# Dealing a weight conversion's steps to an inversion and to the first units by another table (RWKV-7 attention and a hard-swish MLP, one core)

## The chip, the core and the metric

The kernel runs on one core of a Trainium2 chip. It uses the core's five engines: TensorE (PE) for matrix products and transposes, VectorE (DVE) and ScalarE (ACT) for elementwise work, GpSimd (POOL) for some copies and masks, and SyncE (SP), whose queue issues nearly all transfers. Each engine works through its own list of instructions in order, and waits on semaphores for the other engines. The metric is device time in microseconds: 802.33 us, the median of three runs (801.18 to 804.81).

## The reference

Two blocks follow one another. The first is an RWKV-7 recurrence over 768 positions, for 4 batches and 8 heads of width 40; the second is an MLP with the activation h * clip(h + 3, 0, 6) / 6.

```python
for t in range(S):
    y[:, :, t] = np.einsum('bhd,bhde->bhe', rt, state)
    Sa = np.einsum('bhde,bhe->bhd', state, at)
    state_decay = state * wt[:, :, None, :] - np.einsum('bhd,bhe->bhde', Sa, bt)
    state = state_decay + np.einsum('bhd,bhe->bhde', vt, kt)
...
h = x @ w_in                      # x: 3072 x 320, w_in: 320 x 2048
g = h * np.clip(h + 3.0, 0.0, 6.0) / 6.0
out = g @ w_out                   # w_out: 2048 x 320
```

The MLP's two weights are 64-bit floating-point numbers in memory[...]: the kernel rebuilds each weight in float32 from the two 32-bit halves of a double.

## The kernel before, in words

**Units.** Time is cut into blocks of 64 positions. A unit is two such blocks of one half of the batch; there are 24, and four units make a group. For a unit, `prepare` (stages W, gam, A, B, F, K, factor, E, EV) makes decayed inputs and the matrix F of a triangular system. `invert` inverts the triangular blocks of a group on VectorE by 30 rounds of a product (L738) and a sum (L744), then two transposes (L747, L752). `third_block` completes the inverse with products on TensorE (L773, L796), copied out by ScalarE (`zs` L781, `tinv` L806). `step` uses the inverse and carries the state: its stages are RT, VT, C, R, U, UT, H, sn, y, S, rS, and two moves (L995, L1000) that bring the unit's output to the MLP's layout by transfers. In the text "2U" is stage U of unit 2, and "X" and "Y" are the two third blocks of the first group.

**MLP.** `feed_forward` is a stream of products for units whose output has been moved: `expand` (L1051) writes h to two PSUM banks, ScalarE and VectorE make gt of it (L1066, L1067), and `contract` (L1092) multiplies by w_out. Its next part cannot write h before L1067 has read the last one.

**Conversion.** `load_weights` converts 20 pieces (0 to 19). A piece takes four VectorE instructions and two on ScalarE: *mask* L349, then on ScalarE the *pair* L350 and L352, and on VectorE *bits* L369, *join* L373 and, one piece later, *product* L360 with the pair's result. It is a generator: each `next(weights)` emits one of these steps (mask and pair are one). The raw doubles are loaded at L327 into places that come free as earlier pieces are done; a later load is issued at the point of the program where the piece it waits for has been finished.

**Order.** All of it is emitted in one fixed order, with no scheduler: each engine runs its instructions in program order. In the start-up the order comes from two tables. `STEPS` says after which steps of the inversion a step of the conversion is emitted; 47 steps are reached, so larger entries do nothing. `PLAN` lists the stages of the first four units and of X and Y; the number behind a stage is how many conversion steps follow its TensorE instructions, and precede its results on VectorE and ScalarE:

```python
def run(stage, steps=0, mixed=0, deals=0):
    for at in stage:
        if at == DONE:
            return
        aside(steps, mixed)
        deal(deals)
```

Between tables, `while phase[0] == 1: next(weights)` emits a product if the last step emitted was a mask. After the PLAN the second group is prepared and the rest of the run goes on by blocks, with the MLP's stream between the units' stages.

**Buffers.** The products of the stages above go to two-bank PSUM buffers taken in turn: two of the tag `pair` and, until the MLP starts, one of the tag `lent`. A stage's TensorE work waits until the one that had its buffer three turns before has been read. So 3R (L853) takes the buffer of 2U and waits for ScalarE's copy L895 of 2U; the first h takes the place of `lent` and waits for L917 of 2UT.

Of the kernel before, what the change touches and what calls it, by code (L numbers as in the profile page):

```python
# [30 lines left out]
def kernel(  # L31
# [667 lines left out]
    def in_turn(stages, order):  # L699

        for name in order:
            yield from stages[name]()
            shared[0] = None
            yield DONE
# [512 lines left out]
    stages = [step(i) for i in range(NU)]  # L1217
    chains = [in_turn(stages[0], ["RT", "VT", "C", "R"]), in_turn(stages[1], ["RT", "VT", "C"])]
    early = deque(chains[i] for i in (0, 0, 1, 1, 0, 1, 0))
    STEPS = (1, 4, 9, 11, 12, 19, 21, 24, 28, 33, 44, 61, 64)  # L1220
    n, cleared = 0, []
    while not third:
        aside(1)
        if not third:
            n += 1
            if n in STEPS:
                next(weights, None)
# [13 lines left out]
    def block(i, j):  # L1241

        if i % NU < 2:
            if j == 0:
# [3 lines left out]

    PLAN = """X X:1 0U:3 0UT:1 1R
              0sn:1 0H:3 Y:1
              1U 1UT:3 0y:1
              2RT:3 Y:1
              1sn:1 1H:1 2VT:2 0move 0move2
              1y:2 2R
              2S:3 3RT:1
              1move 1move2 2U:2 2UT:1 2C:5
              3R:3 3VT
              2rS:3 2sn:3 2H:4 3S:2  # L1260
              2y:3 3U:2 3UT:7 3C:5
              3rS 3sn:3 3H:3 2move
              3y:2 2move2

              3move
              3move2"""
    BEGIN = 10
    plan = [[x.split(":") for x in line.split()] for line in PLAN.split("\n")]
    chains = {str(i): in_turn(stages[i], [x[0][1:] for line in plan for x in line if x[0][0] == str(i)])
# [182 lines left out]
```

## Time and profile before

| | us |
|---|---|
| median of three runs | 802.33 |
| the profiled execution, its own time | 802.65 |
| its span, first to last instruction | 800.6 |
| TensorE busy (matmuls) | 734.8 |
| VectorE busy | 501.2 |
| ScalarE busy | 306.6 |
| GpSimd busy | 177.0 |
| a conversion step on VectorE: mask, bits (each) | 0.42 |
| join, product (each) | 0.69, 0.68 |
| ScalarE pair, both instructions | 1.47 |

The profile's page gives busy times and the span in slices. The trace answers finer questions: a timeline of one engine in order of time (start, duration, engine, line, operation, output and inputs, count, and in brackets the idle time before it with what ended it), the chain of work that ended last, and tables by window. "PEclk" is the clock granted to TensorE, as a share of full speed. [...]

### The profile page before, as it was taken

What the parts mean: (1) busy time and instruction counts of PE and PEld (TensorE: products, weight loads), DVE (VectorE), ACT (ScalarE), POOL (GpSimd) and SP (SyncE); (2) the same over time, 40 slices, a digit from 0 to 9 for tenths busy, and PEclk for the clock granted to TensorE, in tenths of its full rate; (3) what the DMA queues carried; (4) which work ended last, traced back from release to release, by engine and by line L of the source; (5) the groups of instructions that cost most, each with busy time, mean ns of one, the idle gap of its engine ahead of it and who ended that gap; (6) DMA issues with size and microseconds to landing.
All of it is one profiled execution on the core that took longest, in us unless ns stands there. A gap on an engine that the chain in (4) does not pass through costs nothing.

```text
span 800.6 us, 35291 instructions
## 1 busy us (share of the span) xinstructions
PE 734.8 (92%) x15832; PEld 624.2 (78%) x15832; DVE 501.2 (63%) x986; ACT 306.6 (38%) x648; POOL 177.0 (22%) x318
## 2 busy tenths in 40 slices
PE   5725878999999989999999999999999999999998
PEld 4624766878778868888888888888888888888886
DVE  7898877679555699555698445897444983322210
ACT  2345753321644424553344453324444324412111
POOL 6403012420323222223124123304122202000000
PEclk9955688999999999999999999999999999999999
DMA  9583563420233331233222233213222101110000
GB/s 122 110 190 94 130 165 58 75 49 9 44 57 68 58 57 27 53 65 56 43 44 42 44 59 62 51 30 57 46 49 47 23 18 29 30 25 13 14 19 17
DMA packets 174214, 45.02 MB, mean 56 GB/s; under 512 B 157424, under 2 KB 172784, under 8 KB 174064
## 3 DMA queue, kind: packets, MB, share of 16 engines
q1 hardware_dynamic: 169760, 42.03, 27.7%
q8 instruction: 125, 2.05, 1.1%
q10 hardware_dynamic: 4304, 0.74, 0.7%
q14 instruction: 25, 0.20, 0.1%
HBM read 34.08 MB, written 3.93 MB: 47 GB/s over the span
## 4 chain that ended last, share of the span: by engine, by line
PE 79%; DVE 8%; issue 4%; DMA 3%; SPq 2%; ACT 2%; POOL 1%; DVEq 0%; POOLq 0%; ACTq 0%
PE h L1051 27%; PE o L1092 24%; PE pair L509 4%; PE pair L969 3%; PE one L471 3%; PE pair L946 2%; PE pair L481 2%; PE pair L853 2%; PE pair L891 2%; DVE wm L552 1%; PE pair L687 1%; PE pair L927 1%; SPq L327 1%; PE pair L796 1%; PE pair L911 1%
## 5 line engine op out<-in xcount | busy, mean ns | idle before, releaser
L1051 PE MATMUL h<-xt,win 128*128 128x128 f32 (+1 forms) x2304 | 251.3, 283 | 4.7 <-DVE gt L1067 4.7
L1051 PEld LDWEIGHTS h<-xt,win 128*128 128x128 f32 (+1 forms) x2304 | 231.7, 192 | 21.7 <-DVE gt L1067 5.0
L1092 PE MATMUL o<-wout,gt 128*128 128x320 f32 x768 | 231.5, 445 | 0.0
L1092 PEld LDWEIGHTS o<-wout,gt 128*128 128x128 f32 x768 | 139.1, 191 | 50.7 <-issue 0.8
L1067 DVE SCALAR_TENSOR_TENSOR gt<-gt,h 128x512 f32<-128x512 f32 x96 | 61.9, 680 | 72.5 <-ACT gt L1066 72.1
L1066 ACT ACTIVATE gt<-h,three 128x512 f32<-128x512 f32 x96 | 62.2, 686 | 98.8 <-PE h L1051 98.4
L981 POOL TENSOR_TENSOR yg<-ys,gam 128x512 f32<-128x512 f32 x22 | 39.4, 1792 | 164.5 <-DVE ys L980 72.5
L738 DVE TENSOR_TENSOR prod<-x 128x30 f32<-128x30 f32 (+9 forms) x180 | 67.1, 373 | 8.7 <-POOL x L723 3.3
L660 POOL TENSOR_TENSOR KBt<-K,rgt 128x320 f32<-128x320 f32 x22 | 19.1, 866 | 213.0 <-ACT rgt L649 209.4
L744 DVE TENSOR_TENSOR x<-x,prod 128x30 f32<-128x30 f32 (+9 forms) x180 | 62.2, 345 | 5.4
L954 DVE TENSOR_TENSOR state<-pair,state 40x320 f32<-40x320 f32 (+1 forms) x44 | 21.5, 488 | 64.9 <-PE pair L946 38.6
L517 DVE COPY_PREDICATED score<-mask,pair 128x512 f32<-128x512 int32 x71 | 49.8, 722 | 0.9 <-PE pair L509 0.5
L980 DVE TENSOR_TENSOR ys<-pair,ys 128x512 f32<-128x512 f32 x22 | 15.2, 690 | 43.4 <-PE pair L687 22.0
L552 DVE TENSOR_TENSOR_SCAN wm<-wm,start 128x528 f32<-128x528 f32 x24 | 37.8, 1575 | 0.8
L541 DVE TENSOR_TENSOR_SCAN prods<-wm,start 128x528 f32<-128x528 f32 x24 | 30.2, 1265 | 10.1 <-ACT wm L538 10.1
L969 PE MATMUL pair<-score,KBt 64*64 64x64 f32 x1472 | 29.3, 231 | 4.2 <-DVE state L954 3.1
L831 ACT ACTIVATE RT<-pair 128x512 f32<-128x512 f32 x21 | 12.5, 597 | 52.9 <-PE pair L481 52.9
L692 ACT ACTIVATE EV<-pair 64x320 f32<-64x320 f32 x44 | 19.0, 432 | 34.3 <-PE pair L687 23.7
L969 PEld LDWEIGHTS pair<-score,KBt 64*64 64x64 f32 x1472 | 25.8, 143 | 7.0 <-DVE state L954 3.6
L806 ACT ACTIVATE tinv<-pair 32x256 f32<-32x256 f32 x48 | 18.0, 374 | 31.5 <-PE pair L796 30.9
L569 POOL COPY gam<-prods 128x256 f32<-128x256 f32 x24 | 22.6, 940 | 29.5 <-DVE prods L541 25.7
L1110 ACT ACTIVATE ob<-o 128x320 f32<-128x320 f32 x22 | 9.6, 435 | 49.4 <-PE o L1092 29.6
(262 smaller groups left out, 1060.5 us busy)
## 6 DMA issues: line engine op xcount, KB each, us to landing
V<-in_v_dram SPq DMA_DIRECT2D x96, 40.0 KB
out_dram<-ob SPq DMA_DIRECT2D x47, 80.0 KB
R<-in_r_dram SPq DMA_DIRECT2D x92, 40.0 KB
B<-in_b_dram SPq DMA_DIRECT2D x42, 80.0 KB
K<-in_k_dram SPq DMA_DIRECT2D x42, 80.0 KB
W<-in_w_dram SPq DMA_DIRECT2D x37, 80.0 KB
A<-in_a_dram SPq DMA_DIRECT2D x37, 80.0 KB
xt<-yg SPq DMA_DIRECT2D x72, 40.0 KB
```

Source lines behind the costliest of these rows:

```text
L509: nc.tensor.matmul(out=o[i][half(q), n, :], lhsT=lhs[half(i, D), n ^ (2 * q * swap), half(q)], rhs=rhs[half(i, D), n, half(q)], start=True ...
L517: nc.vector.copy_predicated(out=x[:].rearrange("p (i h) t -> p i h t", i=2), mask=mask8, data=o[2])
L541: nc.vector.tensor_tensor_scan(out=prods[:].rearrange("p r m i -> p (r m i)"), data0=wm[:, 0:SCAN], data1=start[:], initial=0.0, op0=ALU.m ...
L552: nc.vector.tensor_tensor_scan(out=back, data0=back, data1=start[:], initial=0.0, op0=ALU.mult, op1=ALU.add)
L738: nc.vector.tensor_tensor(out=pv, in0=_ap(x[:], (i + 1) * L + i, [[L, n], [0, i]]), in1=_ap(x[:], i * L, [[0, n], [1, i]]), op=ALU.mult,)
L744: nc.vector.tensor_tensor(out=rest, in0=rest, in1=pv, op=ALU.add)
L969: nc.tensor.matmul(out=y[q][half(s), pr, :], lhsT=o[name][half(q), h * D:h * D + SLOT], rhs=m[name][half(q), 4 * rs + 2 * s + j, :], start ...
L981: nc.gpsimd.tensor_tensor(out=yg[:], in0=m["ys"][:].rearrange("p r q t -> p r (q t)"), in1=o["G"][:], op=ALU.mult)
L1051: nc.tensor.matmul(out=hp[c][:, i, :], lhsT=lhsT, rhs=rhs, start=(begun[c] == 0), stop=(begun[c] == 3 * NQ - 1))
L1066: nc.scalar.activation(out=gt[:], in_=hp[c][:], func=AF.Relu, bias=three[:], scale=1.0)
L1067: nc.vector.scalar_tensor_tensor(out=gt[:], in0=gt[:], scalar=6.0, in1=hp[c][:], op0=ALU.min, op1=ALU.mult)
L1092: nc.tensor.matmul(out=op[:], lhsT=gts[c][:, n, :], rhs=wout[:, c * HJ + r * NQ + n, :], start=((split or r == 0) and c == 0 and n == 0), ...
```

## The change

Only the two tables change. The instructions are the same, and on TensorE their order is too; on VectorE and ScalarE, conversion steps stand at other places between the inversion's steps and the first units' results; on SP one load stands at another place.

```diff
-    STEPS = (1, 4, 9, 11, 12, 19, 21, 24, 28, 33, 44, 61, 64)
+    STEPS = (6, 10, 16, 18, 25, 27, 30, 44, 45, 55, 61, 64)
...
-    PLAN = """X X:1 0U:3 0UT:1 1R
-              0sn:1 0H:3 Y:1
-              1U 1UT:3 0y:1
-              2RT:3 Y:1
+    PLAN = """X X:2 0U:4 0UT:2 1R
+              0sn:2 0H:1 Y:2
+              1U 1UT:2 0y
+              2RT:1 Y:1
               1sn:1 1H:1 2VT:2 0move 0move2
               1y:2 2R
-              2S:3 3RT:1
-              1move 1move2 2U:2 2UT:1 2C:5
-              3R:3 3VT
+              2S:3 3RT:2
+              1move 1move2 2U:3 2UT:1 2C:5
+              3R:4 3VT
               2rS:3 2sn:3 2H:4 3S:2
-              2y:3 3U:2 3UT:7 3C:5
-              3rS 3sn:3 3H:3 2move
-              3y:2 2move2
+              2y:3 3U:1 3UT:10 3C:5
+              3rS:1 3sn:2 3H:4 2move
+              3y:1 2move2
```

## The prediction

> **What bounds the kernel now.** I read the page first, then windows, the chain through the start-up, and the engines' timelines there.
>
> ```profile
> PE 734.8 (92%) x15832; PEld 624.2 (78%) x15832; DVE 501.2 (63%) x986; ACT 306.6 (38%) x648; POOL 177.0 (22%) x318
> PE   5725878999999989999999999999999999999998
> PEclk9955688999999999999999999999999999999999
> ```
>
> From slice 8 on (140 us, where the second group is being prepared) TensorE is full. The windows (span, PE, PEld, DVE, ACT, POOL busy, then clock, DMA share, GB/s) say so in microseconds:
>
> ```profile
> 40.00:60.00 20.00, 5.03 (x84) 4.39 (x80) 18.60 (x49) 9.76 (x16) 0.00 (x0) 0.59 0.88 190
> 80.00:100.00 20.00, 16.35 (x460) 14.68 (x460) 16.01 (x33) 14.12 (x25) 0.99 (x3) 0.67 0.54 130
> 100.00:120.00 20.00, 14.34 (x348) 13.20 (x347) 14.86 (x29) 10.15 (x16) 2.25 (x4) 0.84 0.63 165
> 140.00:160.00 20.00, 20.00 (x376) 17.17 (x375) 13.78 (x25) 6.28 (x15) 9.23 (x13) 1.00 0.41 75
> ```
>
> In the first row VectorE inverts, and TensorE has 5.03 us of work. After 120 us TensorE is busy 19.52 us in a mean window of 20. Whatever shifts its start into that stretch, at about 134 us, shifts the end by as much. In front of it the chain, in order of time (start, length, what), runs through the conversion:
>
> ```profile
> 105.21 0.49 DVE state L954
> ...
> 107.57 0.64 DVE score L517
> 108.21 0.57 DVE raw L373
> 109.15 0.73 ACT parts L350
> 109.91 0.72 ACT parts L352
> 110.63 0.48 ACT S L880
> 111.11 0.59 ACT gt L1066
> 111.72 0.70 DVE gt L1067
> 112.46 1.49 PE h L1051 x8
> 113.95 1.96 PE pair L969 x64
> 115.94 0.69 DVE ys L980
> ```
>
> Here is the gate: h was ready at 108.4, but ScalarE has the pair of piece 16 queued in front of 3S and L1066, and waits for its mask on VectorE (L349, 108.70). TensorE idles 4.07 us. After L980 (2y) VectorE runs thirteen conversion steps to 124.5, then the second group's scans. TensorE waits for it once more:
>
> ```profile
> 116.88 1.76 DVE L360 TENSOR_TENSOR wout<-raw,parts 128x512 f32<-128x512 f32 x1
> 133.62 1.99 PE L969 MATMUL pair<-score,KBt 64*64 64x64 f32 x64 [3.06 <-DVE state L954]
> 98.13 1.07 SPq L327 DMA_DIRECT2D raw<-in_moe_w_out_dram  x2
> 111.44 0.57 SPq L327 DMA_DIRECT2D raw_fb<-in_moe_w_out_dram  x1
> ```
>
> These are VectorE, TensorE and SP's queue; the last two are loads of pieces 15 and 16, and of 17.
>
> [...] after the idle of 4.07 us the clock is 0.57 in 113 to 114 us and 0.50 in the next two. [...] between TensorE's stall of 0.66 us at 89.6 and its stall of 2.00 us at 93.5 lie 127 pairs of weight load and product[...], while the transfers are full (share 1.07). [...] the product above, 1.76 us in place of 0.68 while GpSimd runs L981 (116.77 to 118.1).
>
> **The change, step by step.** Nothing is added or removed; by the built order, TensorE's list is unchanged. Conversion steps ahead of each first-unit result in VectorE's list, before and after: L747 12/10; 0sn 19/20; 0H 22/21; 0y 27/25; 1sn 32/28; 1H 33/29; 1y 37/33; 2C 49/47; 3R 52/51; 2sn 58/57; 2H 62/61; L1067 64/63; 2y 67/66; 3C 80/80.
>
> *Step 1, inversion.* A join and a mask leave it. With a join between, L744 to L738 is 0.93 us (50.08 to 51.01), without 0.45; with a mask 0.66. So 0.48 + 0.22 = 0.70; but twice two insertions now share a gap and hide less, about 0.1 each. I take 0.5 earlier (0.3 to 0.7).
>
> *Step 2, X, Y, 0y.* ScalarE's pair of piece 3 (63.03 to 64.5 before, in idle time) now stands between zs and L806: zs 67.0 to 68.5, pair to 69.9, L806 then, against 70.18: 0.3 of the 0.5 is left. The pair of piece 5 no longer delays Y's zs (77.54; Y's products end 0.4 earlier), which held 0y: 0.5 earlier at 0y and, TensorE being continuous but for fetch, to 1y and 2R (L977, 91.00 before, at 90.5). VectorE waits longer for 0y and 1sn, as four fewer conversion steps precede them: bounds 1 to 2.5 us of its time, covered by its slack ahead of 2sn (step 3); beyond that each microsecond costs one.
>
> *Step 3, 2U.* After 2R both orders have bits, join, mask, pair, S, RT: 2C stays 0.5 early (95.5). But now the pair of piece 10 stands between RT and 2U's copy L895: mask 10 ends at 95.3, pair 96.8, L895 97.15 (96.3 before). 3R needs its buffer: 97.2 in place of 96.4, against 96.92. Behind it stand 3VT, h, 2rS, 2sn. So +0.3 from here: the step costs 0.8 (0.3 to 1.3). 2sn ends at 105.4, and L954 starts at 105.5. VectorE, counted by rounds of four (2.0 us each from 95.2, with L517 0.62 and L857 0.40), reaches it at 104.8: no delay, but only 0.7 of slack.
>
> *Step 4, the gate.* From L954 at 105.5: bits, join, mask 15 (to 107.4), product, 2H, bits, join (to 109.6). ScalarE: pair 15 to 108.9, S to 109.4, L1066 to 110.0 and 110.55. Pair 16 comes after. L1067 starts at 110.05, against 111.72: 1.67 earlier; were step 3 free, 2.5. h follows at 110.8, 2y, and L980 at 114.25.
>
> *Step 5, load 16.* On SP it moves behind R and the eight moves of unit 1 (four and eight transfers, 8.3 us from 99.29 to 107.68): issued at 106.7 to 107.2. Loads 15 and 16 were issued from 98.13 and the first 512 KB had passed by about 101.7, by the windows' GB/s; so 3.6 us, landing at about 110.3. The mask of 16 comes at 111.25, and a delay up to 112.9 would still end before L980. Behind it on VectorE: product 15, bits 16, L980. Bounds: 0 to +1.5. I take 0. SP's other transfers (unit 1's moves 0.5 earlier, two loads for the second group 0.5 later) hide under TensorE's queue, which asks for them at about 111 and 123; with that cover gone they cost what they are late, under 1 us.
>
> *Step 6, to the scans.* Before, join 16 ran in the wait ahead of L980; now behind it, so fourteen steps follow: +0.61. From L980 to the last product is 8.57 + 0.61. L981's collision (1.08 before) falls on join, mask and product: between 0.2 and 1.1, taken as 0.7, thus −0.4. End of the conversion: 114.25 + 9.18 − 0.4 = 123.0, against 124.5.
>
> *Step 7, what is late next.* 3UT's copy L917 stands behind pair 19; its buffer is that of the second group's first W transpose pair (124.14), so TensorE idles longer there, nothing more. Scans, gt, 3sn, 3H, 3y move by the same 1.5. The deals behind 3C emit nothing: the twenty pieces are done.
>
> Sum: −1.67 + 0.61 − 0.4 = −1.5 us. The profiled execution, 800.6 and 2.05 around it, 802.65 in all, would take 801.15; the median 802.33 becomes 800.8, as it lies 0.3 below.
>
> **The rivals.** *TensorE stays at full clock.* Its idle before h shrinks from 4.07 to about 2.1 us. At full clock h x8 takes 1.06 and L969 x64 1.09 (as at 225.5 us) for 1.49 and 1.96: L980 1.3 earlier. Load 17, landing about 114.5 (111.44 less 0.5, and 3.6), then holds its mask 0.3: −1.0 more, 799.8. Should the stretch from 82 to 88 also escape its half clock (0.50 granted), 3 us more, 796.8. [...] Against: [...] the fetch stalls stay.
>
> *Half clock lasts[...] longer (slower).* Step 3 lengthens the sparse stretch at 93.5 to 97.2. The clock was 0.50 from 96.5 to 102.5[...]. The gate is then no earlier, join 16 still stands behind L980: +0.2 to +0.6, 802.5 to 802.9. [...] Against: 3R waits 0.8 only.
>
> *Load 16 takes the gate's place.* Past 112.9 each microsecond counts one; landing at 114.4 undoes everything, 802.3. Against: the transfers' share is 0.07 to 0.28 from 104 to 108, so it has the engines to itself.
>
> **How the numbers follow.** Likeliest as summed, 0.50 (own range 799.5 to 801.8); full clock 0.27; half clock 0.13; load 0.10. 0.5% is 4.0 us, about what a measurement of this kernel can tell from no change. Faster by more: half of the full-clock case, 0.14, and 0.04 of the likeliest: 0.18. Slower by more: 0.06 of half clock, 0.04 of the load and 0.02 elsewhere: 0.12. Within: 0.70. The range 797.4 to 803.6 leaves out the far ends of both clock cases.
>
> **What would show it.** L747 at 63.1; 3R about 97.2 with L895 ahead of it; L1067 near 110.1 and TensorE's wait there near 2 us; mask 16 with no wait on a transfer; last product near 123.0; 3y near 132.1. Wrong if VectorE is late for 2sn (the waits at 0y and 1sn then do cost), if the mask of 16 or 17 waits for its load, or if the clock row differs between 80 and 116 us.

## The result, and the profile after

| us | kernel before | changed kernel |
|---|---|---|
| median, run side by side | 803.36 | 800.22 |
| lowest to highest | 800.69 to 805.68 | 797.36 to 801.50 |
| profiled execution, own time | 802.65 | 800.22 |
| its span | 800.6 | 798.4 |

The ratio is 0.996, with a 95% interval from 0.9946 to 0.9974: 3.1 us less. The gain is clear of the noise, and under the 4.0 us that the prediction took as the bound for faster. A repeat on another occasion gave 800.54 us against 803.43, ratio 0.996 (0.9944 to 0.9975).

The page of the changed kernel, the same rows as before (busy times by engine, then TensorE's busy tenths and granted clock in 40 slices):

```profile
PE 727.1 (91%) x15832; PEld 617.9 (77%) x15832; DVE 501.3 (63%) x986; ACT 307.2 (38%) x648; POOL 176.3 (22%) x318
PE   5624676999999989999999999999999999999998
PEclk9855888999999999999999999999999999999999
```

VectorE, ScalarE and GpSimd do what they did. TensorE's busy time fell by 7.7 us, although its instructions are unchanged; a product counts as longer at half clock (in the kernel before, the 24 products of h took 4.79 us from 98.81 us on, with a granted clock of 0.50 to 0.55 up to 103 us, and 2.15 us from 106.25 us on, with 1.00), and the mean granted clock is 0.963 for 0.959. The clock row differs by two tenths in the slice from 80 to 100 us (8 for 6), and by one in that from 20 to 40 us (8 for 9), in which the code is the same. The window from 80 to 100 us (span, PE, PEld, DVE, ACT, POOL busy, then clock, DMA share, GB/s; the clock was 0.67 before):

```profile
80.00:100.00 20.00, 13.06 (x456) 11.58 (x456) 14.93 (x31) 13.32 (x23) 0.99 (x3) 0.85 0.59 140
```

From 140 us on TensorE is full as before (19.67 us of the 20 up to 160), so what counts is how early the second group is ready. The chain of work through the gate:

```profile
106.33 0.49 DVE state L954
...
109.01 0.72 ACT parts L352
109.74 0.48 ACT S L880
110.22 0.59 ACT gt L1066
...
110.83 0.70 DVE gt L1067
...
111.57 1.16 PE h L1051 x8
112.73 1.14 PE pair L969 x64
...
113.89 0.70 DVE ys L980
...
114.64 6.99 DMA raw<-in_moe_w_out_dram
```

ScalarE's pair of piece 15 is followed at once by S and L1066; the pair of piece 16 no longer stands there. Then something new: behind L980 the chain goes into a transfer of raw doubles, that of piece 19, where before it went through thirteen conversion steps. Piece 17 waits for its transfer too. The timelines of the changed kernel show both waits and five other places (VectorE, TensorE, SP's queue; in brackets the idle time before, and what ended it):

```profile
117.25 0.43 DVE L349 TENSOR_SCALAR parts<-raw_fb 128x512 uint32<-128x512 uint32 x1 [2.07 <-DMA raw_fb<-in_moe_w_out_dram]
121.73 0.43 DVE L349 TENSOR_SCALAR parts<-raw 128x512 uint32<-128x512 uint32 x1 [0.38 <-DMA raw<-in_moe_w_out_dram]
97.79 1.09 PE L853 MATMUL pair<-state,at 40*64 40x40 f32 x32 [0.99 <-ACT U L895]
125.13 3.54 PE L1051 MATMUL h<-xt,win 128*128 128x128 f32 x24
133.73 1.34 PE L969 MATMUL pair<-score,KBt 64*64 64x64 f32 x64 [1.25 <-DVE state L954]
135.00 2.42 PE L1092 MATMUL o<-wout,gt 128*128 128x320 f32 x8
108.28 0.52 SPq L327 DMA_DIRECT2D raw<-in_moe_w_out_dram  x1
111.94 1.55 SPq L327 DMA_DIRECT2D raw_fb<-in_moe_w_out_dram  x1
```

Mask 17 (first row) waits 2.07 us for its load, issued at 111.94, and mask 19 another 0.38 us. 3y's L969 waits 1.25 us for 3.06 and takes 1.34 us for 1.99. Listed times of neighbours overlap by up to about 0.1 us (L969 is listed to 135.07 us, the products behind it from 135.00). These eight products of `contract` take 2.42 us; in the kernel before they took 3.14:

```profile
135.54 3.14 PE L1092 MATMUL o<-wout,gt 128*128 128x320 f32 x8
```

**Where the time went.** Clock times of two profiles can't be subtracted here: the first mask on `tinv` starts at 40.60 before, 41.88 after and 40.67 in the repeat, with the same code in front of it, because its load lands sooner or later. So I count from that mask, to milestones up to the scan (L541) that waits 1.32 us for L538, at 141.85 before and 140.59 after.

| stretch (us) | before | predicted change | change | change, repeat |
|---|---|---|---|---|
| first mask to 2sn's L954 | 64.61 | +0.3 | -0.16 | -1.26 |
| L954 to L1067 (the gate) | 6.51 | -1.96 | -2.01 | -2.01 |
| L1067 to 2y's L980 | 4.22 | 0 | -1.16 | -0.23 |
| L980 to the second group's first scan | 9.10 | +0.2 | +2.16 | +1.06 |
| first scan to the later scan | 16.81 | 0 | -1.37 | -1.37 |
| sum | 101.25 | -1.5 | -2.54 | -3.81 |

The two sums stand on either side of the measured 3.1 us. The gate is as forecast; the two rows below L980 are not, and cancel in part. Behind the later scan the profiles are not alike either: 658.7 us remain to the end before, 657.8 and 660.2 in the changed kernel's two, 657.8 to 660.5 in all fourteen. A difference at the scan thus says what the start-up gains, and no profile of one execution says within two microseconds what is left of it at the end.

### The profile page after: what moved, and what is told of

It is laid out like the page before. It is cut to its first block, busy times and chain, and to the rows that moved or that the text cites. A ratio compares the mean times of both kernels' runs of the same rounds, so it can differ in the third digit from the quotient of the medians.

```text
span 798.4 us, 35294 instructions
## 1 busy us (share of the span) xinstructions
PE 727.1 (91%) x15832; PEld 617.9 (77%) x15832; DVE 501.3 (63%) x986; ACT 307.2 (38%) x648; POOL 176.3 (22%) x318
## 3 DMA queue, kind: packets, MB, share of 16 engines
q8 instruction: 125, 2.05, 1.1%
HBM read 34.08 MB, written 3.93 MB: 48 GB/s over the span
## 4 chain that ended last, share of the span: by engine, by line
PE 73%; DVE 13%; issue 5%; SPq 3%; DMA 3%; ACT 2%; POOL 1%; DVEq 0%; POOLq 0%; ACTq 0%
PE h L1051 25%; PE o L1092 22%; PE pair L509 4%; PE pair L969 3%; PE pair L946 2%; DVE prod L738 2%; DVE x L744 2%; PE pair L481 2%; PE one L471 2%; SPq L455 2%; PE pair L853 2%; PE pair L891 2%; DVE prods L541 1%; PE pair L927 1%; DVE wm L552 1%
## 5 line engine op out<-in xcount | busy, mean ns | idle before, releaser
L1092 PE MATMUL o<-wout,gt 128*128 128x320 f32 x768 | 229.6, 442 | 0.0
L1092 PEld LDWEIGHTS o<-wout,gt 128*128 128x128 f32 x768 | 138.1, 190 | 50.4 <-issue 0.2
L1067 DVE SCALAR_TENSOR_TENSOR gt<-gt,h 128x512 f32<-128x512 f32 x96 | 62.0, 681 | 70.5 <-ACT gt L1066 70.5
L1066 ACT ACTIVATE gt<-h,three 128x512 f32<-128x512 f32 x96 | 62.2, 686 | 99.7 <-PE h L1051 99.3
L981 POOL TENSOR_TENSOR yg<-ys,gam 128x512 f32<-128x512 f32 x22 | 39.0, 1772 | 160.3 <-DVE ys L980 73.7
L954 DVE TENSOR_TENSOR state<-pair,state 40x320 f32<-40x320 f32 (+1 forms) x44 | 21.4, 487 | 65.4 <-PE pair L946 39.1
L980 DVE TENSOR_TENSOR ys<-pair,ys 128x512 f32<-128x512 f32 x22 | 15.2, 690 | 40.8 <-PE pair L687 21.8
L541 DVE TENSOR_TENSOR_SCAN prods<-wm,start 128x528 f32<-128x528 f32 x24 | 30.8, 1288 | 10.1 <-ACT wm L538 10.0
L806 ACT ACTIVATE tinv<-pair 32x256 f32<-32x256 f32 x48 | 18.0, 375 | 30.8 <-PE pair L796 30.1
L969 PE MATMUL pair<-score,KBt 64*64 64x64 f32 x1472 | 27.8, 224 | 1.2 <-DVE state L954 1.2
L969 PEld LDWEIGHTS pair<-score,KBt 64*64 64x64 f32 x1472 | 24.5, 137 | 3.8 <-DVE state L954 1.8
```

The costliest lines, as they stand in the source:

```text
L541: nc.vector.tensor_tensor_scan(out=prods[:].rearrange("p r m i -> p (r m i)"), data0=wm[:, 0:SCAN], data1=start[:], initial=0.0, op0=ALU.m ...
L969: nc.tensor.matmul(out=y[q][half(s), pr, :], lhsT=o[name][half(q), h * D:h * D + SLOT], rhs=m[name][half(q), 4 * rs + 2 * s + j, :], start ...
L981: nc.gpsimd.tensor_tensor(out=yg[:], in0=m["ys"][:].rearrange("p r q t -> p r (q t)"), in1=o["G"][:], op=ALU.mult)
L1066: nc.scalar.activation(out=gt[:], in_=hp[c][:], func=AF.Relu, bias=three[:], scale=1.0)
L1067: nc.vector.scalar_tensor_tensor(out=gt[:], in0=gt[:], scalar=6.0, in1=hp[c][:], op0=ALU.min, op1=ALU.mult)
L1092: nc.tensor.matmul(out=op[:], lhsT=gts[c][:, n, :], rhs=wout[:, c * HJ + r * NQ + n, :], start=((split or r == 0) and c == 0 and n == 0), ...
```

## The experiments

Each was timed side by side with the kernel before on one chip, on three occasions on which the kernel before had medians of 803.11, 803.67 and 803.43 us. "From the first mask" is counted as above. One profile of a kernel can't tell differences of about a microsecond: the changed kernel's own two differ by 1.3 us at the later scan.

### The gate by itself, and the gate undone

`gate_alone` is the kernel before with one step moved; `gate_undone` is the changed kernel with that step put back.

```diff
 # gate_alone, from the kernel before
-              2rS:3 2sn:3 2H:4 3S:2
-              2y:3 3U:2 3UT:7 3C:5
+              2rS:3 2sn:3 2H:4 3S:1
+              2y:4 3U:2 3UT:7 3C:5
 # gate_undone, from the changed kernel
-              2rS:3 2sn:3 2H:4 3S:2
-              2y:3 3U:1 3UT:10 3C:5
+              2rS:3 2sn:3 2H:4 3S:3
+              2y:2 3U:1 3UT:10 3C:5
```

> The kernel before with one conversion step moved: mask and pair of piece 16 stand behind L1067 and L1066 and no longer ahead of them. Theory A (the gate makes the gain): L1067 starts about 110.2 in place of 111.72, TensorE's wait ahead of h falls from 4.07 to about 2.5 us, its clock stays full behind it, L980 about 113.2 to 114; the median falls by 2 to 3 us, as much as the whole change. Theory B (the gain comes from the inversion and the first units, the gate's part being swallowed by the wait for load 17): at most 0.7 us faster.

> The changed kernel with that one step put back ahead of L1067 and L1066. Here load 16 comes late (issued near 108), so the mask of 16 now waits for it and L1066 with it. Theory A: L1067 at 112.5 to 113.5, TensorE's wait back at 4 us or more and its clock halved behind it; the gain is gone, between equal to the kernel before and 2 us slower. Theory B: still 2 us or more faster than before.

Measured: `gate_alone` 801.32 us against 803.11, ratio 0.9981 (0.9968 to 0.9994). `gate_undone` 805.10 against 803.11, ratio 1.0023 (1.001 to 1.0036): slower than the kernel before. Timelines of `gate_undone`, VectorE and TensorE:

```profile
110.08 0.43 DVE L349 TENSOR_SCALAR parts<-raw 128x512 uint32<-128x512 uint32 x1 [0.75 <-DMA raw<-in_moe_w_out_dram]
113.10 1.28 DVE L1067 SCALAR_TENSOR_TENSOR gt<-gt,h 128x512 f32<-128x512 f32 x2 [2.60 <-ACT gt L1066]
113.84 2.08 PE L1051 MATMUL h<-xt,win 128*128 128x128 f32 x8 [5.50 <-DVE gt L1067]
```

With pair 16 ahead of L1066 again, mask 16 waits 0.75 us for load 16, which stands at its new place on SP; ScalarE waits for the mask, L1066 behind it, and TensorE for 5.50 us; h behind it takes 2.08 us for 1.16 (the granted clock was 0.64 from 112 to 116 us and 0.51 in the next four, for 1.00 in the changed kernel). So one step is worth 1.8 us in the old order, a little less than the 2 to 3 expected, and about 5 in the new one (2.0 us above the kernel before, where the changed kernel is 3.1 below), where it also keeps load 16's wait out of the gate.

### 3U's copy, which the prediction passed over

The table does one more thing at ScalarE: 3U's copy L895 comes ahead of the pair of piece 17, not behind it. `gate_and_3u` adds that to `gate_alone`.

```diff
 # from the kernel before
-              2rS:3 2sn:3 2H:4 3S:2
-              2y:3 3U:2 3UT:7 3C:5
+              2rS:3 2sn:3 2H:4 3S:1
+              2y:4 3U 3UT:9 3C:5
```

> The kernel before with the step of gate_alone and one more order changed on ScalarE only: the copy L895 of 3U stands ahead of the pair of piece 17. In gate_alone that pair waited for load 17 and held 3U's copy, and TensorE with it, for 4.43 us. Theory A, amended (two ScalarE copies held behind a conversion pair whose data is late): TensorE's wait of 4.43 us goes to under 0.5, its clock stays full, 3y's products take about 1.3 in place of 1.98 us, and the median falls by another 1 to 2 us, to 2.5 to 3.5 under the kernel before, as the whole change does. Theory B (something else in the change makes the rest): as gate_alone, 1.5 us under.

Measured: 801.22 us against 803.67, ratio 0.9971 (0.9955 to 0.9987). The interval overlaps that of `gate_alone`, so the medians show no gain from the copy, where 1 to 2 us more were expected. The traces show a difference of kind. TensorE in `gate_alone`:

```profile
117.76 1.14 PE L509 MATMUL pair<-RT,VT 40*64 40x64 f32 x32 [4.43 <-ACT U L895]
...
122.68 2.15 PE L1051 MATMUL h<-xt,win 128*128 128x128 f32 x24
...
131.52 1.98 PE L969 MATMUL pair<-score,KBt 64*64 64x64 f32 x64 [2.89 <-DVE state L954]
```

Pair 17 waits for mask 17, which waits 2.87 us for load 17; the copy and 3C's L509 wait behind them. TensorE then has work up to the second group, runs the 24 products of h in 2.15 us, is early for 3y and idles 2.89 us there; L969 behind it takes 1.98 us, which nothing covers (the granted clock was 1.00 from 124 to 128 us and 0.65 from 132 to 136). With the copy in front, 3C goes on at once, TensorE idles ahead of the second group's WA transposes instead (6.88 us in `gate_and_3u`, 6.04 in the changed kernel), and the half clock falls on those 24 products (3.92 and 3.54 us, with a granted clock of 0.50 from 124 to 128 us in both, and 1.00 from 132 to 136), which end before VectorE's L954 anyway. From the first scan to the later one this is 15.45 us, for 16.73 in `gate_alone`. The traces agree on it: in the three kernels with the old place of the copy (before, `gate_alone`, `inversion_alone`) h x24 takes 2.15 and the stretch 16.73 to 17.12; in the others h x24 takes 3.08 to 3.93 and the stretch 15.43 to 15.45, except in `parts_and_wa` below. 3y's L969 and the eight products of L1092 behind it account for the whole difference: 1.34 and 2.42 us where the stretch is short, 1.99 and 3.14 before, 1.98 and 3.07 in `gate_alone`, 1.34 and 4.11 in `inversion_alone`.

But the first scan comes 1.25 us later in `gate_and_3u` than in `gate_alone` (82.87 us from the first mask, for 81.62): mask 17 waits 3.17 us for its load, for 2.87, and mask 19 waits 0.72 us for its own, for none. The later scan is where it was, at 98.31 for 98.35. That the copy's new place makes the kernel faster is not shown.

### The inversion's table

```diff
 # inversion_alone, from the kernel before
-    STEPS = (1, 4, 9, 11, 12, 19, 21, 24, 28, 33, 44, 61, 64)
+    STEPS = (6, 10, 16, 18, 25, 27, 30, 44, 45, 55, 61, 64)
-    PLAN = """X X:1 0U:3 0UT:1 1R
+    PLAN = """X X:4 0U:3 0UT:1 1R
```

> The kernel before with the changed STEPS, and the three conversion steps that no longer fall in the inversion (a join, a mask and pair, a product) given to X; from 0U on as before. Prediction's steps 1 and 2 alone: from the first mask to L747 0.4 to 0.5 us less, 0.3 of it left at the copies of X, nothing to 0.5 us at the end. If the inversion made the gain (theory B), 2 us or more faster.

Measured: 802.43 us against 803.67, ratio 0.9986 (0.9968 to 1.0003): 1.2 us less, the interval just reaching no change; it leaves room for the 0 to 0.5 us expected. This and the 1.8 us of `gate_alone` make 3.0, as much as the whole change. L747 comes 22.59 us after the first mask, for 23.01 before.

### The copy of 2U, which was to cost 0.8 us

`pair10_later` puts 2U's copy L895 back ahead of the pair of piece 10.

```diff
 # from the changed kernel
-              1move 1move2 2U:3 2UT:1 2C:5
+              1move 1move2 2U:1 2UT:3 2C:5
```

> The changed kernel with the copy L895 of 2U ahead of the pair of piece 10 on ScalarE again. Step 3 of the prediction: TensorE's wait for L895 ahead of 3R (0.99 us in the changed kernel) goes, 3R and h come 0.8 to 1 us earlier; what is left of it at L1067 is at most 0.5, since VectorE has little slack ahead of 2sn. So 0 to 0.7 us faster than the changed kernel. If 3R's delay was covered altogether, no difference.

Measured: 800.47 us against 803.67, ratio 0.996 (0.9949 to 0.9972), as the changed kernel. TensorE in `pair10_later`:

```profile
96.23 0.84 PE L509 MATMUL pair<-RT,VT 40*64 40x64 f32 x32 [1.61 <-ACT RT L831]
96.82 1.06 PE L853 MATMUL pair<-state,at 40*64 40x40 f32 x32
...
105.36 0.69 PE L509 MATMUL pair<-RT,UT 40*64 40x64 f32 x32 [1.19 <-ACT ys L933]
```

3R's wait of 0.99 us is gone, but 2C in front of it now waits 1.61 us for RT, and further on TensorE waits 1.19 us for ScalarE's ys. L954 of 2sn comes 64.11 us after the first mask, for 64.45 and 63.35 in the changed kernel's two profiles. Another wait ends last, as the expectation allowed.

### The loads

Mask 17's wait is the new item. Three edits of the order on SP's queue test it: load 16 before unit 1's moves (`load16_early`), the second group's transfers of W and A behind loads 17 and 18 (`wa_later`), and both (`loads_both`). `after_rep` is the changed kernel and `wa_later_rep` is `wa_later`, each once more.

```diff
 # load16_early, from the changed kernel
-              1move 1move2 2U:3 2UT:1 2C:5
+              2U:3 1move 1move2 2UT:1 2C:5
 # wa_later, from the changed kernel
-        if t == BEGIN - 2:
+        if t == BEGIN - 1:
             seconds()
             for name in "WA":
                 fetch(name, NU + 1)
+        if t == BEGIN - 2:
             third.clear()
```

> The changed kernel with unit 1's two moves behind stage 2U on the PLAN's line, so that load 16 stands ahead of the eight moves on SP. The mask of 16 loses its wait of 0.30 us; it was covered by the wait for 2y, so theory A expects the time of the changed kernel within 0.5 us, and unit 1's moves 0.6 us later at no cost. If the position of load 16 matters more than that (its traffic ahead of 2sn or of the instruction fetches), it shows as over 1 us either way.

> The changed kernel with the four transfers of W and A for the second group's second unit (and the two GpSimd fills ahead of them) issued one PLAN line later, behind loads 17 and 18. Theory A (what is left is held by load 17, whose mask waited 2.07 us in the changed kernel): load 17 is issued near 109 in place of 111.94, its mask waits under 0.3 us, the last product ends about 122.5 in place of 124.6, 3y comes 1.5 to 2 us earlier, and the median is 1.5 to 2 us under the changed kernel's, some 4.5 to 5 under the kernel before. Theory B (the conversion's end does not set the time): within 0.5 us of the changed kernel.

> The changed kernel with load 16 ahead of unit 1's moves and the second group's W and A behind loads 17 and 18. Masks 16 and 17 should not wait (0.86 and 0.67 us in the kernel with the second edit alone). If the waits for loads set the end of the conversion, that end comes 0.5 to 1 us earlier than with either edit alone and the median is 1 to 2 us under the changed kernel's; if not, as the changed kernel within 0.5 us.

> The changed kernel once more, as the ruler for the other three of this series. By the earlier result 0.996 of before (0.9946 to 0.9974).

> The changed kernel with W and A of the second group fetched behind loads 17 and 18, once more. If the wait of mask 17 for its load (2.07 us) is what kept step 6 from its 1.5 us, mask 17 waits under 1 us, the conversion ends 0.5 to 1 us earlier from the first mask, and the time is 0.5 to 1 us under the repeated changed kernel. If TensorE only waits for something else then, the two agree within 0.3 us.

| kernel | median, before | ratio (95%) | wait of mask 16 | wait of mask 17 | first mask to first scan |
|---|---|---|---|---|---|
| changed kernel | 800.22, 803.36 | 0.9960 (0.9946 to 0.9974) | 0.30 | 2.07 | 83.27 |
| `after_rep` | 800.54, 803.43 | 0.9960 (0.9944 to 0.9975) | 0.12 | 0.99 | 82.00 |
| `load16_early` | 799.70, 803.11 | 0.9945 (0.9924 to 0.9967) | 0 | 1.86 | 82.52 |
| `wa_later` | 799.40, 803.11 | 0.9935 (0.9912 to 0.9958) | 0.86 | 0.67 | 82.35 |
| `wa_later_rep` | 801.00, 803.43 | 0.9969 (0.9956 to 0.9981) | 1.62 | 0 | 83.24 |
| `loads_both` | 800.14, 803.67 | 0.9957 (0.9943 to 0.9972) | 0 | 0 | 81.91 |

Load 16's new place costs nothing that these intervals can tell. `wa_later` looked better and in the repeat did not: there mask 17's wait is gone, but mask 16 waits 1.62 us: its load goes out 0.5 us later and takes 4.9 us to use, for 4.1 in the changed kernel, now with loads 17 and 18 right behind it. The wait had only moved. `loads_both`, in which neither mask waits, was to be 1 to 2 us under the changed kernel if the waits for loads set the end of the conversion; its ratio is the changed kernel's (0.9957 for 0.9960). None of these beats the changed kernel beyond doubt, and what the waits for loads cost the whole kernel is not shown by any of them.

### The parts joined

`parts_joined` is the kernel before with the inversion's table, the gate and 3U's copy, and the old deals between X and 2H. `parts_and_wa` has W and A behind loads 17 and 18 besides.

```diff
 # parts_joined, from the kernel before
-    STEPS = (1, 4, 9, 11, 12, 19, 21, 24, 28, 33, 44, 61, 64)
+    STEPS = (6, 10, 16, 18, 25, 27, 30, 44, 45, 55, 61, 64)
-    PLAN = """X X:1 0U:3 0UT:1 1R
+    PLAN = """X X:4 0U:3 0UT:1 1R
...
-              2rS:3 2sn:3 2H:4 3S:2
-              2y:3 3U:2 3UT:7 3C:5
+              2rS:3 2sn:3 2H:4 3S:1
+              2y:4 3U 3UT:9 3C:5
 # parts_and_wa: this, and the edit of wa_later
```

> The inversion's table, the gate and 3U's copy alone, with the old deals between X and 2H. If the gains of the parts add up (1.2 and 2.45 us), 0.9955 of before, 3.6 us less, and a little under the changed kernel; then the deals between X and 2H cost about 0.5 us. If the earlier inversion only makes mask 17 wait longer for its load, the parts do not add: no better than the gate with 3U's copy, 0.997, and the wait of mask 17 is above 3.17 us.

> The same three parts, with W and A fetched behind loads 17 and 18. If load 17 is what limits them, mask 17 waits under 1 us and the time is 0.5 to 1.5 us below the three parts alone, 0.994 of before or less, under the changed kernel. If not, as the three parts alone.

Measured: `parts_joined` 800.31 us against 803.43, ratio 0.9959 (0.9944 to 0.9973), the same as the whole change: the other deals add nothing that can be measured. VectorE and SP in `parts_joined`:

```profile
111.74 0.68 DVE L980 TENSOR_TENSOR ys<-pair,ys 128x512 f32<-128x512 f32 x1
116.76 0.43 DVE L349 TENSOR_SCALAR parts<-raw_fb 128x512 uint32<-128x512 uint32 x1 [4.33 <-DMA raw_fb<-in_moe_w_out_dram]
112.13 0.58 SPq L327 DMA_DIRECT2D raw_fb<-in_moe_w_out_dram  x1
```

L980 comes 69.61 us after the first mask, for 75.34 before and 72.01 in the changed kernel, and then mask 17 waits 4.33 us for load 17. In all kernels where mask 17 waits and W and A go out ahead of load 17 (the changed kernel and its repeat, `gate_alone`, `gate_and_3u`, `load16_early`, `parts_joined`) it starts 74.1 to 75.4 us after the first mask, however early VectorE is: waits from 0.99 to 4.33 us. The load is a floor to all of them. In `parts_and_wa`, VectorE, TensorE and SP:

```profile
112.57 0.42 DVE L349 TENSOR_SCALAR parts<-raw_fb 128x512 uint32<-128x512 uint32 x1
118.88 0.43 DVE L349 TENSOR_SCALAR parts<-raw 128x512 uint32<-128x512 uint32 x1 [1.14 <-DMA raw<-in_moe_w_out_dram]
130.89 1.83 PE L969 MATMUL pair<-score,KBt 64*64 64x64 f32 x64 [1.72 <-DVE state L954]
108.08 0.53 SPq L327 DMA_DIRECT2D raw_fb<-in_moe_w_out_dram  x1
```

Load 17, issued at 108.08, holds nothing; mask 17 starts 70.87 us after the first mask, mask 19 waits 1.14 us for its load, and the first scan comes at 80.60 for 83.10. Then the later scan follows 16.85 us behind it for 15.44, 3y's L969 and the eight products behind it being slow (1.83 and 3.34), so 1.1 us of 2.5 is left. The median is 798.92 us of six runs, ratio 0.9938 (0.992 to 0.9956): faster than the kernel before, and the lowest median here, but the interval overlaps that of the changed kernel. Whether it beats that one is not shown.

## Why the prediction was right, and where it was not

The time (800.8 forecast, 800.22 measured) held, and so did a change within 0.5%. The gain did not come as near: -1.5 us was forecast, and -3.1 measured side by side. The forecast started from 802.33, the median of three runs, where thirteen gave 803.36; that 1.0 us, which hides part of the miss, is chance. Of the three signs that the prediction named for being wrong two came true: masks 16 and 17 waited for their loads, and the clock row differs between 80 and 116 us. The third, VectorE late for 2sn, is not seen in the changed kernel's first profile, where it waits 0.56 us, but in the repeat it reaches L954 with no wait left (step 3). By its steps:

- **What bounds the kernel**: held. The differences at the later scan follow the medians within about a microsecond: `gate_undone` +1.4 us there and +2.0 in the median, `gate_alone` -2.9 and -1.8, the changed kernel -2.5 and -3.8 in its two profiles and -3.1 and -2.9, `parts_and_wa` -3.8 and -4.5.
- **Step 1**: held. L747 is 0.43 us earlier from the first mask, in the range of 0.3 to 0.7.
- **Step 2**: in part. The pair of piece 3 took 0.36 of that 0.43 from X's L806, not 0.2 of 0.5. Yet L977 of 1y (91.00 before) came 1.2 and, in the repeat, 1.7 us earlier from the first mask, not 0.5: TensorE's clock from 80 to 88 us was 0.90 to 1.00 in both, and 0.50 before. The clock does not explain it, as `gate_alone`, with the old tables there, had 1.00 and 0.87, and its L977 came only 0.3 us earlier. With the old tables L977 is at 50.1 to 50.4 us from the first mask, with the new inversion at 48.6 to 50.1; why by so much is open.
- **Step 3**: the mechanism held. L895 of 2U stands behind pair 10, and 3R waits for it 0.99 us (0.8 forecast). That its removal gains anything fell with `pair10_later`: RT and ys end last there. Steps 1 to 3 together were to bring L954 0.3 us later. From the first mask it is at 64.6, 63.4 and 63.5 with the old deals and the old inversion, at 62.0, 62.4 and 63.0 with the new inversion alone, and at 63.4 to 64.7 with all the new deals but those of one or two edited places. The means are 63.8, 62.5 and 64.1: net +0.3, but as -1.3 from the inversion and +1.6 from the deals, both larger than -0.5 and +0.8. The deals' part lies between 1y's L977 and L954: 14.6 to 15.3 us with the new deals, 13.0 to 14.2 with the old. By the prediction's own count VectorE has 24 conversion steps there for 21, about 1.5 us more at 2.0 us for four, and in five of the eight profiles with the new deals it does not wait ahead of L954. So the slack that was to cover this is used up; no run tests it by itself, and what makes the inversion's part larger is open. TensorE also stalls, for 0.2 to 3.1 us at one to four places between 78 and 97 us, with no instruction to wait for, and these stalls vary from profile to profile as much. There are 37 of them in the fourteen profiles. The three in the kernel before and the three in the changed kernel's first profile end 1.5 to 1.6 us after a transfer of 16 KiB ends on the queue that the page lists as "instruction" (before: a transfer from 92.73 to 94.04 us, and a stall to 95.52), which fits the prediction's reading of them as fetch.
- **Step 4**: held to 0.1 us. L954 to L1067 is shorter by 2.01 (1.96 forecast), and TensorE's wait is 2.06 us (2.1). `gate_alone` and `gate_undone` show it to be the change's main part. Behind it came the rival of full clock, where the likeliest case left 4.2 us as it was: h and L969 took 1.16 us each (the granted clock was 1.00 from 108 to 116 us), and L980 came another 1.16 earlier. The repeat, with the same wait of 2.07, kept 0.23 of that: h took 1.26 and L969 1.99 us, and its clock was 0.77 from 108 to 112 us and 0.80 in the next four. So the shorter wait was followed by either clock and did not assure the gain; what decides between the two is not shown, and the 0.27 for this rival was my estimate.
- **Step 5**: held but for 0.3 us. Load 16 went out at 108.28, which from the first mask is 66.4 us, as forecast (66.1 to 66.6). Mask 16 waited 0.30 us for it, and L980 did not.
- **Step 6** is the one that failed. L980 to the last product's end was to take 9.18 - 0.4 = 8.8 us and took 10.7, and 9.6 in the repeat. Join 16 behind L980 was there: where no mask waits, in `pair10_later` and `loads_both`, the stretch takes the 9.18 of the fourteen steps. The 0.4 taken off for L981's collision did not come there: mask 17 took 1.50 us for 0.42, which is 1.08 more, as the product beside L981 did before (1.76 for 0.68). In the changed kernel L981 runs from 114.72 to 116.32 us, most of it in VectorE's wait for mask 17 from 115.18 to 117.25, and no conversion step there takes over 0.69 us. And loads 17 and 19 had no term in the sum: masks 17 and 19 waited 2.07 and 0.38 us for them, in the repeat 0.99 and 0.35. The full-clock rival gave load 17 3.6 us from issue to use, and 0.3 us of wait. It was issued when forecast (70.1 us from the first mask, for 70.3), but usable only 5.3 us later; in the repeat 5.5 us. One microsecond of that is the issue itself, which takes 1.55 and 1.71 us on SP, for 0.57 before; what makes it longer is open. In the four other kernels in which mask 17 waits behind the four transfers of W and A, the issue takes 0.57 or 0.58 us and the load is usable after 4.4 to 4.6. What W and A cost is mostly the place in SP's list: with them ahead (`parts_joined`) load 17 goes out 70.0 us after the first mask and mask 17 waits 4.33 us, with them behind (`parts_and_wa`) it goes out at 66.4 and mask 17 does not wait.
- **Step 7** said that TensorE would idle longer ahead of the WA pair, "nothing more". It idles 6.04 us there, and something more follows: the half clock falls on covered products (0.50 granted from 124 to 128 us, for 1.00 before), and 3y's L969 and the eight products behind it run at full clock (1.00 from 132 to 140 us, for 0.70 and 0.87 in its two halves before), 0.65 and 0.72 us less. That is the whole of the 1.37 us to the later scan. The term was left out, with the place of 3U's copy that goes with it.

So the sum was near in part by luck: behind L980 the conversion took 2.0 and, in the repeat, 0.9 us more than forecast, for the loads that the sum lacked, against 1.4 us at 3y and 0.2 to 1.2 us at the gate that it also lacked. The half-clock and the load-16 rivals did not occur: around the 24 products of h ahead of 2sn the half clock lasts 6.8 us in the changed kernel's first profile (97.4 to 104.2), as in the kernel before (96.1 to 102.9). What the half-clock rival would cost was my estimate, which no run here shows.

## What to carry to other kernels

An engine that is made earlier soon meets a transfer that nobody had waited for: list, for each load behind the improved place, when it is issued and how long it takes from issue to use at that place, its issue included (4.4 to 5.5 us for load 17, where an earlier stretch had given 3.6). Where engines run their lists in order, look for every small copy that a neighbour waits for and that stands behind a long step with a wait of its own; moving one step at the gate was worth 1.8 to 5 us. And where TensorE must idle, look at which products stand behind the idle. Here TensorE idled 3.93 to 8.27 us ahead of the second group's WA transposes in eleven profiles, and the 24 products of h behind them took 3.08 to 3.93 us; in the other three it idled there for at most 0.54 us, and they took 2.15. With these covered products behind the idle, the stretch up to the later scan was 1.3 to 1.7 us shorter, though no median shows a gain from that alone.

## What the runs showed that was not expected

- The start varies: the first mask waits 0.97 to 2.8 us for its load in profiles of kernels with the same code ahead of it. Differences of that size must be counted from a common event.
- An idle of 2.05 to 2.07 us in front of h was followed by full clock in three profiles (1.00 granted from 108 to 116 us; h and L969 1.16 us each) and by slower products in three (granted 0.57 to 0.80 from 112 to 116 us; h x8 1.16 to 1.41 us, L969 1.67 to 1.99); behind idles of 4.07 and 5.50 us h was slow in all three profiles that had them (granted 0.50 to 0.64 from 112 to 116 us; h x8 1.49 to 2.08 us).
- An idle of 6.88 us in `gate_and_3u` cost nothing at the later scan (98.31 us from the first mask, for 98.35 in `gate_alone`), as the half clock then fell on the 24 products of h (3.92 us; 0.50 granted from 120 to 128 us) and 3y's L969 took 1.33 us for 1.98.
- With W and A ahead of it, load 17 is usable 4.4 to 5.5 us after its issue begins; load 16, ahead of them in the changed kernel, 4.1 (108.28 to 112.42).
